# Routing weights of a sinkhorn mixture of experts: the maximum over partitions by two small DMAs, the 1e-9 kept inside the table, and the first output pair's steps spread out

## The chip, the cores and the metric

The kernel runs on one core of a Trainium2 chip. A core has TensorE (PE in the profile; its weight loads are the row PEld), VectorE (DVE), ScalarE (ACT), GpSimd (POOL) and the sync engine (SP), whose queue issues DMAs. Each engine works through its own queue in order and waits on semaphores for the others. SBUF is the on-chip memory of 128 partitions; PSUM holds what TensorE writes, in banks of 512 fp32 values per partition. The metric is the device time of one execution in microseconds, the median of the runs; lower is better.

## The reference, cut to what matters

Attention with a sorted key and value order comes first; its output `x` (3072 tokens of 512) goes through eight experts, each token's outputs weighted by a table `P` that is balanced by rows and columns eight times.

```python
def _moe_ref(x, w_gate, w1, w2):
    N, D = x.shape
    E = w_gate.shape[1]
    logits = x @ w_gate
    logits = logits - logits.max()
    P = np.exp(logits)
    for _ in range(8):
        P /= P.sum(1, keepdims=True) + 1e-09
        P /= P.sum(0, keepdims=True) + 1e-09
        P *= N / E
    out = np.zeros((N, D), dtype=np.float32)
    for e in range(E):
        h = np.maximum(x @ w1[e], 0.0)
        ye = h @ w2[e]
        out += P[:, e:e + 1] * ye
    return out.astype(np.float32)
```

N is 3072, E is 8, the hidden width F is 1024. The maximum is over all tokens and experts, and each column sum over all tokens, so both cross the 128 partitions.

## The kernel before

The attention of four batches comes first and lasts until some 123 us. Its matmuls are mixed with those of expert 0, which is computed densely: `expert_hidden` and `expert_out` (line 377) make the unweighted output of expert 0 for a batch's tokens and copy it from PSUM into `osbl`, the output table of 24 tiles of 128 tokens (line 386: tiles 1, 4 and 5 by ScalarE, the others by VectorE). `logits` leaves the gate's logits in `glog`, 128 partitions by 24 tiles by 8 experts.

Then the seven other experts run in a main loop over rounds `r` (line 818). They use a seven-product scheme for 2x2 blocks (Strassen's, in Winograd's form): sums of weight blocks (`sum_w`, `sum_w2`, on GpSimd), of token blocks (`sum_x`) and of hidden blocks (`Pair.sums`, line 702, on GpSimd) are made beforehand. A round has seven steps of the hidden layer, `p1, p5, p6, p2, p7, p3, p4` from `hidden`, each two matmuls of 512 columns (line 601), with copies and relus on ScalarE and two relu-sums on VectorE (line 590, a custom operation). From `r = 5` on a round also has the output steps of a pair of token tiles: `q5, q1, q6, q2, q3` of this round's pair, and `q7, q4` of the pair before, each four matmuls of 256 columns (line 712) and, apart from q1, which is copied by ScalarE (line 723), followed by a `gather` on VectorE (line 662) that multiplies by the routing weight in `glog` and adds to `osbl`. Round 5 is the first with a pair and has no pair before it: the list of its output steps leaves the missing ones out, so its five steps stand behind the first five hidden steps. In rounds 0 to 4 the loop takes the steps of `last_dense` instead: the second half of the last batch's expert 0.

The routing weights come from the generator `balance` (line 550), woven into this. Its table `G` of 192 values per partition lies in PSUM, in the third bank of the ring `oacc`. The maximum of all logits is taken per partition on VectorE (line 558), turned into a row by an fp32 matmul with an identity (559), reduced again (561) and spread to all partitions by a second fp32 matmul with ones (563); then ScalarE takes the exponential (566). Each of eight iterations has a row part on VectorE (572 to 576: sum, add 1e-9, reciprocal, multiply, and the partition's column sums) and a column part: an fp32 matmul with ones that adds over the partitions (578), then on VectorE scale and add (579), reciprocal (581), multiply (582). Every `yield` ends a step.

The order is written by hand. `pin` keeps an instruction at its place on its engine. The string on line 792 says in which order the steps of the dense part (T), of the chain (C) and of `sum_x` (X) are issued before the main loop: a T is one hidden block of 384 tokens (four matmuls, line 776), or half of an output tile (four matmuls, line 784). In the main loop line 862 says behind which hidden steps of rounds 0 to 4 the chain takes a step, and line 849 empties it at round 5. `scale0` (line 753) multiplies a tile of `osbl` by expert 0's weight on ScalarE; it needs the finished `glog`. Line 864 does it for tiles 4 and 0 in round 4; the next tiles follow from round 5 on, two a round.

The output is stored by SP's queue, and only in the last expert (line 667).

Of the kernel before, what the change touches and what calls it, by code (L numbers as in the profile page):

```python
# [13 lines left out]
F32 = mybir.dt.float32  # L14
BF16 = mybir.dt.bfloat16
AF = mybir.ActivationFunctionType
AX = mybir.AxisListType
ALU = mybir.AluOpType


def mkap(t, dims, off=0):
    return bass.AP(tensor=t.tensor, offset=t.offset + off, ap=dims)
# [3 lines left out]
def kernel(  # L26
# [11 lines left out]
    nc = tc.nc  # L38
    B, H, S, D = 4, 8, 768, 64
    NB, BL = 8, 96  # L40
    N, Dm, E, F = 3072, 512, 8, 1024
    NT = 24
# [16 lines left out]
    pin = tc.keep_in_program_order  # L59
# [4 lines left out]
    osbl = xtp.tile([128, NT, Dm], F32)  # L64
    glog = xtp.tile([128, NT, E], F32)
# [21 lines left out]
    def load_w1(e):  # L87
        w1t[e] = wp.tile([128, 4, F], BF16, name="w1e")
        pin(nc.gpsimd.dma_start(out=w1t[e],
                                in_=moe_w1[e].rearrange("(kk k) f -> k kk f", k=128)))  # L90
# [6 lines left out]
    Ibig = ones.tile([128, 128], BF16)  # L97
# [279 lines left out]
    def expert_out(c0, hTs, bank):  # L377
        for tt in range(3):
            oacc = bank()
            for fb in range(8):  # L380
                pin(nc.tensor.matmul(oacc, hTs[:, fb, tt * 128:(tt + 1) * 128],  # L381
                                     w2t[0][:, fb, :], start=(fb == 0), stop=(fb == 7)))
                if fb == 3:
                    yield
            t = c0 // 128 + tt
            (nc.scalar.copy if t in (1, 4, 5) else nc.vector.tensor_copy)(osbl[:, t, :], oacc)
            yield

    def expert0(bb, bank):
# [24 lines left out]
    with tc.tile_pool(name="ps0", bufs=7, space=bass.MemoryType.PSUM,  # L414
# [28 lines left out]
        for eng, i0, n in ((nc.vector.tensor_copy, 0, 5), (nc.scalar.copy, 5, 3)):  # L443
# [3 lines left out]
                                 axis=AX.X))  # L447
# [7 lines left out]
        for h in range(0, 8, 2):  # L455
            nc.vector.tensor_tensor(
                out=Rt[0][:, h:h + 2],
                in0=mkap(pbps, [pbps.ap[0], [1, 2], [32, 8], [0, 16]], off=h),
                in1=mkap(mask16, [mask16.ap[0], [0, 2], [0, 8], [1, 16]]), op=ALU.mult)
# [34 lines left out]
    mpc, xcp, wq, wcq = late("mpc", 1), late("xcp", 1), late("wq", 2), late("wcq", 1)  # L494
# [38 lines left out]
    def sum_x(p, eng, hold=pin):  # L533
        ta, tb = (slice(1024 * p + 512 * i, 1024 * p + 512 * i + 512) for i in range(2))
        b11, b12, b21, b22 = (xtT[:, k:k + 2, t] for k in (0, 2) for t in (ta, tb))
        x1, x2, x4 = (xc[:, j, :, 512 * p:512 * p + 512] for j in range(3))
        for a, b, c in ((b12, b11, x1), (b22, x1, x2), (b21, x2, x4), (b22, b12, b12)):
            for k in ((slice(0, 1), slice(1, 2)) if p == 2 and c is b12 else (slice(0, 2),)):
                hold(eng.tensor_tensor(out=c[:, k], in0=a[:, k], in1=b[:, k],
                                       op=ALU.subtract))  # L540
                yield

    onesc = mpc.tile([128, 128], F32)
    nc.gpsimd.memset(onesc, 1.0)
    I128 = mpc.tile([128, 128], F32)
    nc.scalar.copy(I128, Ibig)
    for _ in sum_x(0, nc.vector, lambda ins: ins):
        pass

    def balance():  # L550

        room = rings["oacc"][2]
        G = room[:, 0:NT * E].rearrange("p (t e) -> p t e", e=E)
        sums = room[:, 192:192 + NT]
        csps = room[:, 256:256 + E]
        gmps = room[:, 384:512]
        gm = mpc.tile([128, 1], F32)
        pin(nc.vector.reduce_max(out=gm, in_=glog.rearrange("p t e -> p (t e)"), axis=AX.X))
        pin(nc.tensor.matmul(gmps[0:1, :], gm, I128, start=True, stop=True))
        gm1 = mpc.tile([1, 1], F32)  # L560
        pin(nc.vector.reduce_max(out=gm1, in_=gmps[0:1, :], axis=AX.X, negate=True))
        yield
        pin(nc.tensor.matmul(csps[:, 0:1], onesc[0:1, :], gm1, start=True, stop=True))
        gneg = mpc.tile([128, 1], F32)
        pin(nc.vector.tensor_copy(gneg, csps[:, 0:1]))
        pin(nc.scalar.activation(out=G, in_=glog, func=AF.Exp, bias=gneg))
        rs2 = mpc.tile([128, NT], F32)
        cs2 = mpc.tile([128, E], F32)
        cs1 = mpc.tile([128, E], F32)
        yield  # L570
        for it in range(8):
            pin(nc.vector.reduce_sum(out=sums, in_=G, axis=AX.X))
            pin(nc.vector.tensor_scalar_add(rs2, sums, 1e-9))
            pin(nc.vector.reciprocal(out=rs2, in_=rs2))
            pin(nc.vector.tensor_mul(G, G, mkap(rs2, [rs2.ap[0], rs2.ap[1], [0, E]])))
            pin(nc.vector.reduce_sum(out=cs2, in_=G.rearrange("p t e -> p e t"), axis=AX.X))
            yield
            pin(nc.tensor.matmul(csps, onesc, cs2, start=True, stop=True))
            pin(nc.vector.tensor_scalar(out=cs1, in0=csps, scalar1=float(E) / N,
                                        scalar2=1e-9 * E / N, op0=ALU.mult, op1=ALU.add))  # L580
            pin(nc.vector.reciprocal(out=cs1, in_=cs1))
            pin(nc.vector.tensor_mul(glog if it == 7 else G, G,
                                     mkap(cs1, [cs1.ap[0], [0, NT], cs1.ap[1]])))
            yield

    TOP = 3.0e38
    relu = lambda o, x: nc.scalar.activation(out=o, in_=x, func=AF.Relu)  # L587
# [165 lines left out]
    def scale0(ts):  # L753
        for t in ts:
            pin(nc.scalar.activation(out=osbl[:, t, :], in_=osbl[:, t, :], func=AF.Copy,
                                     scale=glog[:, t, 0:1]))

    def last_dense():
# [7 lines left out]
        for c in range(2):  # L766
# [14 lines left out]
            for tt in range(3):  # L781
# [7 lines left out]
                yield  # L789

    dense, chain, xs = last_dense(), balance(), sum_x(2, nc.vector)
    for step in "TTCXTTCXTTCXTTCTTCTTT":
        next({"T": dense, "C": chain, "X": xs}[step])
    held_x = mpc.tile([128, 2], BF16)
    pin(nc.gpsimd.tensor_copy(held_x, xc[:, 2, 0, 1024:1026]))
# [16 lines left out]
    for m, o in enumerate(ends):  # L812
        e, p, hT, _ = chunks[-1]
# [4 lines left out]
    for r in range(len(pairs) + 6):  # L818
        n, i = r // 4, r % 4
        if n < C:  # L820
            e, p, hT, s3 = chunks[n]
            if i == 0 and (n == 1 or n > 1 and p == 0) and e + 1 < E:
                load_w1(e + 1)
                queue.append(sum_w(e + 1))
            if r == 5 or p == 1 and i == 2 and n > 1 and e + 1 < E:
                load_w2(2 if r == 5 else e + 1)
            if r == 8 or p == 1 and i == 2 and n > 1 and e + 1 < E:
                queue.append(sum_w2(2 if r == 8 else e + 1))
            steps, rest = hidden(e, p, i, hT, s3, r < 4)
        else:  # L830
            steps, spares, rest = spares[:7], spares[7:], None
        k = r - 5
        if k + 1 in range(len(pairs)):
            pairs[k + 1].sums()
        weights((0, 2, 2, 0, 0)[r] if r < 5 else 2 if r < 12 else 1 + i % 2)
        now = pairs[k] if k in range(len(pairs)) else None
        if r < 5:
            outs = [lambda: next(dense), None, lambda: next(dense), None,
                    lambda: next(dense)]
        else:  # L840
            outs = [getattr(a, b) for a, b in
                    ((now, "q5"), (before, "q7"), (now, "q1"), (before, "q4"),
                     (now, "q6"), (now, "q2"), (now, "q3")) if a]
        if now and now.last:
            plains, steps = iter(steps), []
            outs = [next(plains) if o == "x" else getattr(before if o[1:] else now, "q" + o[0])
                    for o in "5 7' x 1 x 4' 6 x 2 x 7 x x 3 4".split()]
            now = None
        if r == 5:
            for _ in chain:  # L850
                pass
        for j in range(max(len(steps), len(outs))):
            if j < len(steps):
                steps[j]()
                if j == 3 and n < C:
                    if k + 1 in range(1, 12):
                        scale0([8 * ((k + 1) // 4) + (k + 1) % 4 + 4 * m for m in range(2)])
                    if k + 1 in range(len(pairs)):
                        pairs[k + 1].keep()
            if j < len(outs) and outs[j]:  # L860
                outs[j]()
            if r < 5 and j != 3 and (6 * r + j - (j > 3)) % 4 < 2:
                next(chain, 0)
            if r == 4 and j in (2, 5):
                scale0([4 if j == 2 else 0])
            if j == 1 and late:
                late()
                late = None
            if r in (6, 7) and j == 6:
                next(xs)  # L870
        late, before = rest, now
        if n >= C and not spares and not before:
            break
# [30 lines left out]
```

## Time and profile before

| what | us |
|---|---|
| median of 3 runs (lowest, highest) | 664.87 (664.72, 664.96) |
| the profiled execution, its own time | 665.08 |
| span of that execution in the trace | 663.3 |

| engine, over the span | busy us | instructions |
|---|---|---|
| TensorE | 646.5 | 4970 |
| VectorE | 475.1 | 909 |
| ScalarE | 386.8 | 758 |
| GpSimd | 465.8 | 430 |

| stretch, us of the span | TensorE busy | VectorE busy | ScalarE busy | GpSimd busy |
|---|---|---|---|---|
| 121 to 134 (maximum, first iterations, dense) | 12.89 | 7.78 | 5.36 | 3.69 |
| 134 to 162 (rounds 0 to 4) | 27.73 | 20.07 | 20.04 | 21.87 |
| 162 to 168.5 (round 5) | 6.41 | 3.87 | 5.23 | 6.24 |
| 168.5 to 175 (round 6) | 6.45 | 4.72 | 4.94 | 6.34 |

All times in the stretch are from the start of the span. The granted clock of TensorE is 1.00 in all four stretches. A line of a timeline gives the start, the duration, the engine, the line of the kernel, the operation, what it writes and reads with its shape, and how many like it were merged. Matmuls are pipelined: the end of one is modelled and overlaps the next, so gaps on TensorE are read from start to start. A few matmul records are missing from a trace.

### The profile page before, as it was taken

To read this page: it belongs to the slowest core of one execution; us is meant where nothing else is said; L and a number is where in the kernel's file an instruction comes from. 1 tells how busy PE (TensorE), PEld (TensorE's weight loads), DVE (VectorE), ACT (ScalarE), POOL (GpSimd) and SP (SyncE) were. 2 spreads that over 40 slices of the span, in tenths; PEclk is the share of its full clock that TensorE was granted. 3 is DMA by queue.
4 is the path that set the end of the run, shared out by engine and by line. 5 is a ranking of instruction groups with operands and counts; after the bars stand their busy time and mean duration, and the time that the engine had idled before them with its cause. 6 is when DMAs were issued, how large, how long until landed. Compare 5 with 4: busy or idle time off the path is not lost.

```text
span 663.3 us, 13065 instructions
## 1 busy us (share of the span) xinstructions
PE 646.5 (97%) x4970; PEld 422.5 (64%) x5047; DVE 475.1 (72%) x909; ACT 386.8 (58%) x758; POOL 465.8 (70%) x430
## 2 busy tenths in 40 slices
PE   5999999999999999999999999999999999999997
PEld 2555565555666666666666666666666666666665
DVE  7846566666777777777777777777777777777775
ACT  5877657476777755555555555555555655555540
POOL 3543540196999898779796979698797969846641
PEclk9999999999999999999999999999999999999999
DMA  9998944004303040120303040302103040000224
GB/s 151 184 220 138 196 72 65 1 1 71 58 1 64 1 65 1 26 40 3 61 1 65 1 64 2 65 1 38 27 1 64 1 65 2 1 1 33 96 81 174
DMA packets 33743, 36.52 MB, mean 55 GB/s; under 512 B 2064, under 2 KB 27088, under 8 KB 33680
## 3 DMA queue, kind: packets, MB, share of 16 engines
q0 software_dynamic: 26448, 26.81, 25.9%
q1 hardware_dynamic: 6832, 8.38, 4.4%
q8 instruction: 39, 0.64, 0.4%
q10 hardware_dynamic: 400, 0.49, 0.2%
q14 instruction: 24, 0.20, 0.1%
HBM read 52.45 MB, written 6.29 MB: 89 GB/s over the span
## 4 chain that ended last, share of the span: by engine, by line
PE 95%; issue 1%; DVE 1%; ACT 1%; ACTq 0%
PE oacc L712 38%; PE bk L601 36%; PE bank L381 5%; PE bank L368 5%; PE bank L220 1%; PE bank L261 1%; PE oacc L784 1%; PE bk L678 1%; PE bank L243 1%; PE bank L196 1%; PE bk L776 1%; PE bank L146 1%; PE oacc L776 1%; PE bk L784 1%; PE bank L181 0%
## 5 line engine op out<-in xcount | busy, mean ns | idle before, releaser
L662 DVE SCALAR_TENSOR_TENSOR osbl<-oacc,glog,osbl 128x256 f32<-128x256 f32 (+1 forms) x411 | 219.2, 534 | 125.0 <-PE oacc L712 115.7
L587 ACT ACTIVATE hT<-bk 128x512 bf16<-128x512 f32 (+1 forms) x176 | 104.2, 592 | 147.5 <-PE bk L601 130.1
L601 PE MATMUL bk<-xtT,w1e 128*128 128x512 bf16 x478 | 143.5, 379 | 0.9
L712 PEld LDWEIGHTS <-hs 128*128 128x128 bf16 x984 | 96.3, 98 | 62.9 <-issue 0.3
L712 PEld LDWEIGHTS <-hT 128*128 128x128 bf16 x904 | 88.4, 98 | 57.9 <-issue 0.6
L702 POOL TENSOR_TENSOR hs<-hT 128x512 bf16<-128x512 bf16 x82 | 95.1, 1159 | 39.9 <-DVE hT L590 34.4
L712 PE MATMUL oacc<-w2e,hT 128*128 128x256 bf16 x764 | 114.6, 273 | 0.6
L702 POOL TENSOR_TENSOR hs<-hs,hT 128x512 bf16<-128x512 bf16 x82 | 94.6, 1154 | 6.4
L702 POOL TENSOR_TENSOR hs<-hT,hs 128x512 bf16<-128x512 bf16 x82 | 94.6, 1153 | 6.4
L601 PE MATMUL bk<-xc,wc 128*128 128x512 bf16 x317 | 95.2, 379 | 0.1
L712 PE MATMUL oacc<-w2e,hs 128*128 128x256 bf16 x616 | 92.4, 273 | 0.7
L601 PEld LDWEIGHTS <-w1e 128*128 128x128 bf16 x672 | 65.8, 98 | 11.6 <-issue 0.3
L590 DVE CUSTOM_DVE_ANT_0 hT<-bk,p 128x512 bf16<-128x512 f32 x84 | 58.1, 691 | 7.7 <-PE bk L601 3.1
L636 ACT COPY p<-bk 128x512 f32<-128x512 f32 x84 | 49.2, 585 | 24.3 <-PE bk L601 21.0
L630 ACT COPY u<-bk 128x512 f32<-128x512 f32 x84 | 49.2, 586 | 22.2 <-PE bk L601 19.5
L621 ACT COPY bk<-bk 128x512 f32<-128x512 f32 x84 | 48.0, 572 | 20.5 <-PE bk L601 20.5
L590 DVE CUSTOM_DVE_ANT_0 hT<-bk,u 128x512 bf16<-128x512 f32 x84 | 57.1, 680 | 1.6 <-PE bk L601 0.6
L712 PE MATMUL oacc<-w2s,hs 128*128 128x256 bf16 x368 | 55.2, 273 | 0.3
L601 PEld LDWEIGHTS <-wc 128*128 128x128 bf16 x504 | 49.3, 98 | 8.0 <-issue 0.2
L655 DVE SCALAR_TENSOR_TENSOR s<-bk,hT 128x512 bf16<-128x512 f32 x80 | 54.4, 680 | 0.0
L601 PE MATMUL bk<-xtT,wc 128*128 128x512 bf16 x160 | 48.2, 379 | 0.4
L601 PE MATMUL bk<-xc,w1e 128*128 128x512 bf16 x158 | 47.8, 379 | 0.0
(140 smaller groups left out, 827.9 us busy)
## 6 DMA issues: line engine op xcount, KB each, us to landing
w2e<-in_moe_w_dram POOLq DMA_DIRECT2D x8, 1024.0 KB, 9.5
w1e<-in_moe_w_dram POOLq DMA_DIRECT2D x7, 1024.0 KB, 8.3
out_dram<-osbl SPq DMA_DIRECT2D x21, 256.0 KB, 2.0
vsb<-vs SPq DMA_DIRECT2D x25, 96.0 KB, 3.3
vt<-in_v_dram POOLq DMA_DIRECT2D x3, 768.0 KB, 12.3
qt<-in_q_dram POOLq DMA_DIRECT2D x4, 384.0 KB, 10.5
kt<-in_k_dram POOLq DMA_DIRECT2D x4, 384.0 KB, 12.3
kt<-in_k_dram POOLq DMA_DIRECT2D x2, 768.0 KB, 14.4
```

What stands on the lines that cost most here:

```text
L368: pin(nc.tensor.matmul(hps[:, 0:n], w1t[0][:, kk, fb * 128:(fb + 1) * 128], xtT[:, kk, c0:c0 + n], start=(kk == 0), stop=(kk == 3)))
L381: pin(nc.tensor.matmul(oacc, hTs[:, fb, tt * 128:(tt + 1) * 128], w2t[0][:, fb, :], start=(fb == 0), stop=(fb == 7)))
L587: relu = lambda o, x: nc.scalar.activation(out=o, in_=x, func=AF.Relu)
L590: return nc.vector._custom_dve(TENSOR_ADD_SAT, out=o, in0=x, in1=y, s0=TOP, s1=0.0)
L601: pin(nc.tensor.matmul(ps, wa[:, kk, :], xa[:, kk, :], start=(first and kk == 0), stop=(kk == 1), skip_group_check=True))
L621: pin(nc.scalar.copy(t["w"], t["u"]))
L630: pin(nc.scalar.copy(t["u2"], t["u"]))
L636: pin(nc.scalar.copy(t["p5"], t["v"]))
L655: pin(nc.vector.scalar_tensor_tensor(out=s3[:, i, :], in0=t["w"], scalar=0.0, in1=c12, op0=ALU.max, op1=ALU.subtract))
L662: pin(nc.vector.scalar_tensor_tensor(out=o, in0=ps, scalar=glog[:, t, e:e + 1], in1=o, op0=ALU.mult, op1=ALU.add))
L702: pin(nc.gpsimd.tensor_tensor(out=s[:, c], in0=a, in1=b, op=o))
L712: pin(nc.tensor.matmul(ps, h[:, fb, :], w[:, fb, :], start=(first and fb == 0), stop=(fb == 3), skip_group_check=True))
```

## The change

The maximum over partitions no longer goes through TensorE: one DMA on SP's queue writes the 128 partial maxima as a row into one partition, VectorE reduces it, and a second DMA spreads the result to 128 partitions. The identity `I128` goes.

The table in PSUM gets a ninth column that holds 1e-9 and a 25th row that holds 1e-9/128, set once. The row sums run over nine columns, the column sums over 25 rows, so the two additions go as separate instructions. The factor N/E moves into the multiplication by the column's reciprocal, now a scalar_tensor_tensor. The `yield` behind the column part goes: a step is now a column part with the next row part.

The order changes with it: a new string before the main loop, one chain step behind every fourth hidden step in rounds 0 to 3, expert 0's tiles 16 and 17 copied by ScalarE, and the scaling of tile 0 in round 5 instead of round 4. Round 5's output steps keep the places that they have in later rounds, with empty places for the missing ones.

```diff
-            (nc.scalar.copy if t in (1, 4, 5) else nc.vector.tensor_copy)(osbl[:, t, :], oacc)
+            (nc.scalar.copy if t in (1, 4, 5, 16, 17) else nc.vector.tensor_copy)(osbl[:, t, :], oacc)
...
-    I128 = mpc.tile([128, 128], F32)
-    nc.scalar.copy(I128, Ibig)
...
-        G = room[:, 0:NT * E].rearrange("p (t e) -> p t e", e=E)
-        sums = room[:, 192:192 + NT]
+        GE = room[:, 0:(NT + 1) * (E + 1)].rearrange("p (t e) -> p t e", e=E + 1)
+        G = GE[:, 0:NT, 0:E]
         csps = room[:, 256:256 + E]
-        gmps = room[:, 384:512]
         gm = mpc.tile([128, 1], F32)
-        pin(nc.vector.reduce_max(out=gm, in_=glog.rearrange("p t e -> p (t e)"), axis=AX.X))
-        pin(nc.tensor.matmul(gmps[0:1, :], gm, I128, start=True, stop=True))
+        gmr = mpc.tile([1, 128], F32)
         gm1 = mpc.tile([1, 1], F32)
-        pin(nc.vector.reduce_max(out=gm1, in_=gmps[0:1, :], axis=AX.X, negate=True))
-        yield
-        pin(nc.tensor.matmul(csps[:, 0:1], onesc[0:1, :], gm1, start=True, stop=True))
         gneg = mpc.tile([128, 1], F32)
-        pin(nc.vector.tensor_copy(gneg, csps[:, 0:1]))
-        pin(nc.scalar.activation(out=G, in_=glog, func=AF.Exp, bias=gneg))
...
+        pin(nc.vector.reduce_max(out=gm, in_=glog.rearrange("p t e -> p (t e)"), axis=AX.X))
+        pin(nc.sync.dma_start(out=gmr, in_=gm))
+        pin(nc.vector.memset(GE[:, 0:NT, E:E + 1], 1e-9))
+        pin(nc.vector.memset(GE[:, NT, 0:E], 1e-9 / 128))
         yield
+        pin(nc.vector.reduce_max(out=gm1, in_=gmr, axis=AX.X, negate=True))
+        pin(nc.sync.dma_start(out=gneg, in_=mkap(gm1, [gm1.ap[0], [0, 128], [1, 1]])))
+        yield
+        pin(nc.scalar.activation(out=G, in_=glog, func=AF.Exp, bias=gneg))
         for it in range(8):
-            pin(nc.vector.reduce_sum(out=sums, in_=G, axis=AX.X))
-            pin(nc.vector.tensor_scalar_add(rs2, sums, 1e-9))
+            pin(nc.vector.reduce_sum(out=rs2, in_=GE[:, 0:NT], axis=AX.X))
             pin(nc.vector.reciprocal(out=rs2, in_=rs2))
             pin(nc.vector.tensor_mul(G, G, mkap(rs2, [rs2.ap[0], rs2.ap[1], [0, E]])))
-            pin(nc.vector.reduce_sum(out=cs2, in_=G.rearrange("p t e -> p e t"), axis=AX.X))
+            pin(nc.vector.reduce_sum(out=cs2, in_=GE[:, :, 0:E].rearrange("p t e -> p e t"),
+                                     axis=AX.X))
             yield
             pin(nc.tensor.matmul(csps, onesc, cs2, start=True, stop=True))
-            pin(nc.vector.tensor_scalar(out=cs1, in0=csps, scalar1=float(E) / N,
-                                        scalar2=1e-9 * E / N, op0=ALU.mult, op1=ALU.add))
-            pin(nc.vector.reciprocal(out=cs1, in_=cs1))
-            pin(nc.vector.tensor_mul(glog if it == 7 else G, G,
-                                     mkap(cs1, [cs1.ap[0], [0, NT], cs1.ap[1]])))
-            yield
+            pin(nc.vector.reciprocal(out=cs1, in_=csps))
+            pin(nc.vector.scalar_tensor_tensor(
+                out=glog if it == 7 else G, in0=G, scalar=float(N) / E,
+                in1=mkap(cs1, [cs1.ap[0], [0, NT], cs1.ap[1]]), op0=ALU.mult, op1=ALU.mult))
...
-    for step in "TTCXTTCXTTCXTTCTTCTTT":
+    for step in "CXXTTTTCXTTCTTTTCTTTC":
...
+        elif r == 5:
+            outs = [now.q5, None, now.q1, None, now.q6, now.q2, now.q3]
...
-            if r < 5 and j != 3 and (6 * r + j - (j > 3)) % 4 < 2:
+            if r < 4 and j != 3 and (6 * r + j - (j > 3)) % 4 == 3:
                 next(chain, 0)
-            if r == 4 and j in (2, 5):
-                scale0([4 if j == 2 else 0])
+            if (r, j) in ((4, 2), (5, 2)):
+                scale0([4 if r == 4 else 0])
```

## The prediction

> **What bounds the kernel now.** I read the shares and the chain of waits first, then the timelines of TensorE (PE), VectorE (DVE) and ScalarE (ACT) from 121 to 175 us, the stretch the diff touches, then the DMA issues.
>
> ```profile
> PE 646.5 (97%) x4970; PEld 422.5 (64%) x5047; DVE 475.1 (72%) x909; ACT 386.8 (58%) x758; POOL 465.8 (70%) x430
> ...
> PE 95%; issue 1%; DVE 1%; ACT 1%; ACTq 0%
> ```
>
> PE is busy 97% and is 95% of the chain that ends last. After 168 us its timeline shows no gap but missing records (one 512-column matmul, 0.216 us, at a time). So time counts only if it leaves PE's own queue, and what PE gains before 168 us it keeps to the end. Four kinds of loss stand in the stretch. First, the fp32 matmuls that spread the logits' maximum:
>
> ```profile
> 123.66 1.46 PE L776 MATMUL bk<-xtT,w1e 128*128 128x384 bf16 x8
> 125.05 0.38 PE L559 MATMUL oacc<-I,gm 128*1 128x128 f32 x2
> 125.36 1.48 PE L776 MATMUL bk<-xtT,w1e 128*128 128x384 bf16 x8
> 126.77 0.38 PE L563 MATMUL oacc<-gm,onesc 1*128 1x1 f32 x2
> 127.08 2.77 PE L776 MATMUL bk<-xtT,w1e 128*128 128x384 bf16 x16
> ```
>
> A 384-column matmul starts every 0.1625 us (16 in 127.08 to 129.69). Eight from 123.66 would end at 124.96; the next group starts at 125.36, so L559 costs 0.40. The same way L563 costs 127.08 - 126.66 = 0.42.
>
> Second and third, PE waiting for the routing chain on DVE, and the chain's length:
>
> ```profile
> 139.98 0.15 DVE L579 TENSOR_SCALAR cs<-oacc 128x8 f32<-128x8 f32 x1
> 140.17 0.20 DVE L581 RECIPROCAL cs<-cs 128x8 f32<-128x8 f32 x1
> 140.41 0.37 DVE L582 TENSOR_TENSOR oacc<-oacc,cs 128x192 f32<-128x192 f32 x1
> 140.81 0.37 DVE L572 TENSOR_REDUCE oacc<-oacc 128x24 f32<-128x192 f32 x1
> 141.21 0.18 DVE L573 TENSOR_SCALAR rs<-oacc 128x24 f32<-128x24 f32 x1
> 141.42 0.30 DVE L574 RECIPROCAL rs<-rs 128x24 f32<-128x24 f32 x1
> 141.76 0.37 DVE L575 TENSOR_TENSOR oacc<-oacc,rs 128x192 f32<-128x192 f32 x1
> 142.16 0.36 DVE L576 TENSOR_REDUCE cs<-oacc 128x8 f32<-128x192 f32 x1
> ...
> 142.57 0.39 PE L578 MATMUL oacc<-cs,onesc 128*128 128x8 f32 x2
> ```
>
> PE's previous group (141.64, four of 384 columns) ended at 142.29; L578 starts 0.05 after L576 ends. PE lost 0.28 here and 0.07 before the L578 at 146.34.
>
> Fourth, the first output pair (round r = 5 of the main loop):
>
> ```profile
> 162.56 0.60 PE L712 MATMUL oacc<-w2s,hs 128*128 128x256 bf16 x4
> 163.21 0.59 PE L601 MATMUL bk<-xc,wc 128*128 128x512 bf16 x2
> 163.81 0.60 PE L712 MATMUL oacc<-w2e,hT 128*128 128x256 bf16 x4
> 164.24 0.59 PE L601 MATMUL bk<-xc,wc 128*128 128x512 bf16 x2
> 164.85 0.60 PE L712 MATMUL oacc<-w2s,hs 128*128 128x256 bf16 x4
> ```
>
> Four of 256 columns take 0.435, two of 512 take 0.43. Gaps: 0.21 before 163.21, 0.17 before 163.81, 0.18 before 164.85, and 0.18 before 167.63: 0.74 in sum. Rounds from r = 6 on, which have seven output steps instead of five packed to the front, have none.
>
> **The change, part by part.**
> *Maximum by two DMAs.* Both fp32 matmuls leave PE: 0.40 + 0.42 = **0.82 gained**; nothing replaces them on PE. What hides the DMAs: on DVE two 0.69 copies (t = 16, 17) leave, one of them ahead of the logits' copy, so the maximum is ready some 0.5 earlier, near 122.7. In the built program's order the exp stands on ACT behind the sixth relu of the dense group. That group ends at 123.66 + 6 x 0.65 = 127.56; a relu starts 0.21 after its group and takes 0.49, so the exp cannot start before 128.26. From 122.7 the two DMAs, a 0.28 reduction (L561's row) and about 0.15 of issue and wake-up have 5.1 us for the pair. The rows:
>
> ```profile
> vsb<-vs SPq DMA_DIRECT2D x25, 96.0 KB, 3.3
> ...
> P<-in_sort_net_dram SPq DMA_DIRECT2D x1, 8.0 KB, 1.6
> glog<-in_moe_w_gate_dram SPq DMA_DIRECT2D x1, 16.0 KB, 1.8
> ```
>
> The new ones move 512 bytes in 4-byte pieces. Nearest are 8 KB (1.6) and 16 KB in 32-byte pieces (1.8); upper row 3.3, SBUF to SBUF. I take 1.8 each: 3.6 of 5.1, hidden. At 3.3 each the exp is 1.5 late; the relus of groups seven and eight queue behind it, and the chain is late too; the first column matmul has 0.3 slack, so PE would lose 1.2. On SP's queue the last earlier DMA was issued near 95 us and the output stores come hundreds of us later: nothing is queued behind. On DVE the second reduction waits for the first DMA with one sum_x operation behind it, which the held-over copy on POOL (130.23 before) follows; it comes earlier, near 126.
>
> *Copies t = 16, 17 on ACT.* 2 x 0.59 into ACT's 5.62 us idle before 124.56: nothing. Without that cover the first relu would be up to 0.6 late. The removed cast of I128 (0.315 on ACT at 105) gets no credit.
>
> *The 1e-9 in the table.* Column and row sums take it along; L573 and L579 go, the factor N/E moves into a scalar_tensor_tensor. From L579 to the end of L576 an iteration is 2.54 us (130.08 to 132.62). Without the pitches of L579 (0.19) and L573 (0.22) it is 2.13. The sums run over 216 and 200 elements instead of 192; by the copies L386 (512 elements, 0.69) and L281 (48, 0.20) an element costs 1.06 ns, so +0.03: 2.16. The last multiply keeps 0.37, as L655 (same operation, 512, 0.68) minus 320 elements gives 0.34. The rows of G are now 9 apart; L576 already reads with a step of 8 and takes 0.36, as the contiguous L572. With 0.32 from the matmul's start to DVE's next operation (135.47 to 135.79) and 0.05 back, a loop from matmul to matmul is 2.53.
>
> *Steps merged and spaced.* Column and next row part are one step now. I counted PE's work between the eight column matmuls in the built order (0.15 each). From first to second 12 x 0.216 = 2.59, slack to the loop 0.2; to the third 4.32, ample; to the fourth 8 x 0.216 + 0.65 = 2.38, slack 2.38 + 0.15 - 2.53 = 0: a tie; to the fifth 3.46; sixth 4.11; seventh 2.59, slack 0.2; eighth 3.89. Following DVE as well: in round 1 the relu-sum (L590, 0.69) that frees p4's bank stands behind a whole 2.16 step, and PE reaches p4 some 0.14 early. New waits I take as 0.09 + 0.14 = 0.23 against 0.35 before: **0.1 gained**. Bounds: with 0.03 off each of the six operations the new waits vanish (gain 0.35); with 0.05 on each, five places wait, 1.2 in all (loss 0.85).
>
> *Round 5.* q1 waits for q5's gather, p-steps wait for ACT copies; the gather and copies get a whole 0.43 step more between them, and the scaling of tile 0 (L755, 0.72) leaves round 4, where it stood ahead of the relu at 162.57. It needs glog from the chain, whose last step ends in round 3 now. Following ACT, 0.1 of the 0.74 stays: **0.63 gained**; bounds 0 and 0.74. POOL must keep up: pair 1's sums (L702) ended at 167.20, used at 168.49, slack 1.29, more than the 0.63; and the relu-sum that released POOL at 157.95 no longer waits behind a row part. Without that cover the next pair's q5 would wait the difference.
>
> Sum: 0.82 + 0.10 + 0.63 = 1.55. The profiled execution was 665.08 (span 663.3 and 1.8 around it), the median 664.87: 0.2 apart. Span 661.75, profiled 663.5, median **663.3**.
>
> **Rivals.**
> A. *Merged steps dearer.* DVE operations on the 9-step table cost 0.05 more each, or the merged step blocks relu-sums longer: 0.82 - 0.85 + 0.63 = 0.6 gained, 664.3. For: two slacks of 0.2 and a tie; a 0.05 change decides. Against: L576 pays nothing for its step.
> [...]
> B. *Spacing idle.* Round 5's waits come from ACT's load (5.23 of the 6.5 us from 162), not from the order, and stay: 0.92 gained, 663.95.
> C. *Slower: the DMAs on one engine.* If the 128 4-byte pieces go one after another, at the mean packet of SP's queue (4.4% of 16 engines' 663.3 us over 6832 packets, 0.068 us), each DMA is 1.6 + 8.7 = 10.3. PE waits 20.6 - 5.4 = 15, time near 678. It eats the whole gain from a pair of 5.4 + 1.55 = 7.0 us on. For: no DMA like it runs here. Against: the 16 KB row's 512 pieces of 32 bytes landed in 1.8.
> [...]
> D. *No new waits at all*: 0.82 + 0.35 + 0.74 = 1.91, 662.95.
>
> **How the numbers follow.** Forecast 0.45, D 0.15, A 0.17, B 0.13, C 0.05, and 0.05 for a loss of more than 0.2% by some chain wait. The likeliest one's own range is 663.0 to 663.9. The range reaches from below D to A with dearer operations and 3.3 us DMAs: 662.6 to 665.0. What a measurement of this kernel can tell from no change, 0.2%, is 1.33 us. Below 663.54 lie D and most of the forecast's share: 0.58; within it A, B and the rest: 0.35; slower than 666.2: 0.07.
>
> **What would show it.** No fp32 matmul among the first eight dense groups, which then last 5.2 us; both DMAs landing in about 2 us and the exp following the sixth relu at once; PE gaps only near the fourth column matmul and p4 of round 1, together below 0.3; round 5 about 5.2 us long with gaps of 0.1. Wrong if ACT's exp waits for the DMA, if the six DVE rows exceed 0.37, or if round 5 keeps its gaps.

## The result and the profile after

The changed kernel takes 662.92 us (median of 9 runs, 662.54 to 664.29), the kernel before 665.06 beside it (9 runs, 664.58 to 665.93): a ratio of 0.9969, 95% interval 0.9960 to 0.9978. The profiled execution took 662.94 with a span of 661.2, against 665.08 and 663.3.

The page after, with the busy times and the engine shares of the chain that ended last:

```profile
PE 648.5 (98%) x5043; PEld 421.9 (64%) x5043; DVE 471.2 (71%) x892; ACT 388.1 (59%) x759; POOL 466.0 (70%) x430
...
PE 96%; DMA 2%; POOL 1%; DVE 0%; issue 0%; POOLq 0%
```

TensorE was the bound and still is. Its busy time is higher although two matmuls went, because fewer records are missing from this trace (5043 for 4970, beside 5043 and 5047 weight loads). What can be compared is a stretch from start to start: from the first dense group (L776 before, now L773) to the first output step of round 6. It was 44.83 us (123.66 to 168.49) and is 42.79 (123.69 to 166.48): 2.04 us shorter, and from there to the end both kernels differ by 0.1.

The timeline of the changed kernel at the maximum (start, duration, engine, line, operation):

```profile
122.46 0.35 DVE L561 TENSOR_REDUCE gm<-glog 128x1 f32<-128x192 f32 x1
123.69 5.36 PE L773 MATMUL bk<-xtT,w1e 128*128 128x384 bf16 x32
124.84 0.27 DVE L566 TENSOR_REDUCE gm<-gmr 1x1 f32<-1x128 f32 x1 [0.49 <-DMA gmr<-gm]
127.79 0.49 ACT L584 ACTIVATE hT<-bk 128x384 bf16<-128x384 f32 x1 [0.16 <-PE bk L773]
128.18 0.42 ACT L569 ACTIVATE oacc<-glog,gneg 128x192 f32<-128x192 f32 x1
128.89 1.89 PE L781 MATMUL bk<-w2e,hT 128*128 128x512 bf16 x8
```

All 32 matmuls of the dense block now run without a break, and the next group starts 5.20 after the first. The exp (L569) follows the sixth relu at once. Its bias came by the two DMAs; their issues and landing times, from the views by tile:

```profile
L562 SPq DMA_DIRECT2D gmr<-gm x1: 548/548/548, 122.8 to 122.8; - x1
...
DMA to landing us min/median/max: 2.0/2.0/2.0
L567 SPq DMA_DIRECT2D gneg<-gm x1: 549/549/549, 125.1 to 125.1; - x1
...
DMA to landing us min/median/max: 2.4/2.4/2.4
```

The second was issued at 125.1 and landed near 127.5, 0.6 to 0.7 before the exp could start anyway.

The timeline of the changed kernel around the fourth column matmul, TensorE and VectorE:

```profile
139.89 0.59 PE L598 MATMUL bk<-xc,wc 128*128 128x512 bf16 x2
139.95 0.37 DVE L574 TENSOR_REDUCE cs<-oacc 128x8 f32<-128x200 f32 x1
140.23 0.68 DVE L587 CUSTOM_DVE_ANT_0 hT<-bk,u 128x512 bf16<-128x512 f32 x1
140.37 0.39 PE L577 MATMUL oacc<-cs,onesc 128*128 128x8 f32 x2
...
140.83 0.20 DVE L578 RECIPROCAL cs<-oacc 128x8 f32<-128x8 f32 x1
141.06 0.37 DVE L579 SCALAR_TENSOR_TENSOR oacc<-oacc,cs 128x192 f32<-128x192 f32 x1
141.46 0.38 DVE L571 TENSOR_REDUCE rs<-oacc 128x24 f32<-128x216 f32 x1
141.88 0.30 DVE L572 RECIPROCAL rs<-rs 128x24 f32<-128x24 f32 x1
142.22 0.37 DVE L573 TENSOR_TENSOR oacc<-oacc,rs 128x192 f32<-128x192 f32 x1
142.62 0.37 DVE L574 TENSOR_REDUCE cs<-oacc 128x8 f32<-128x200 f32 x1
142.90 0.68 DVE L587 CUSTOM_DVE_ANT_0 hT<-bk,p 128x512 bf16<-128x512 f32 x1
143.20 0.59 PE L598 MATMUL bk<-xtT,wc 128*128 128x512 bf16 x2
143.64 0.59 PE L598 MATMUL bk<-xc,w1e 128*128 128x512 bf16 x2
```

The iteration has six VectorE operations and is 2.16 long (140.83 to 142.99). PE waits 0.05 before L577 and at no other column matmul; p4 (143.64) follows p3's group of 143.20 without a gap, since the relu-sum that frees its bank (started at 142.90) ended 0.06 before.

Round 5, TensorE alone:

```profile
161.24 0.60 PE L709 MATMUL oacc<-w2s,hs 128*128 128x256 bf16 x4
161.68 1.06 PE L598 MATMUL bk<-xc,wc 128*128 128x512 bf16 x4
162.58 0.60 PE L709 MATMUL oacc<-w2e,hT 128*128 128x256 bf16 x4
163.01 1.03 PE L598 MATMUL bk<-xtT,w1e 128*128 128x512 bf16 x4
163.88 0.60 PE L709 MATMUL oacc<-w2s,hs 128*128 128x256 bf16 x4
...
166.48 0.60 PE L709 MATMUL oacc<-w2s,hs 128*128 128x256 bf16 x4
```

From 161.24 to 166.48 it is 5.24 long; of the 0.74 of gaps 0.04 is left.

### The profile page after: what moved, and what is told of

Its sections match the earlier page's. It is cut to its first block, busy times and chain, and to the rows that moved or that the text cites. A ratio compares the mean times of both kernels' runs of the same rounds, so it can differ in the third digit from the quotient of the medians.

```text
span 661.2 us, 13122 instructions
## 1 busy us (share of the span) xinstructions
PE 648.5 (98%) x5043; PEld 421.9 (64%) x5043; DVE 471.2 (71%) x892; ACT 388.1 (59%) x759; POOL 466.0 (70%) x430
## 4 chain that ended last, share of the span: by engine, by line
PE 96%; DMA 2%; POOL 1%; DVE 0%; issue 0%; POOLq 0%
PE bk L598 38%; PE oacc L709 38%; PE bank L381 5%; PE bank L368 5%; DMA kt<-in_k_dram 2%; PE bank L220 1%; PE bank L261 1%; PE oacc L781 1%; PE bk L675 1%; PE bank L243 1%; PE bank L196 1%; PE oacc L773 1%; PE bk L773 1%; PE bank L146 1%; PE bk L781 1%; PE bank L181 0%
## 5 line engine op out<-in xcount | busy, mean ns | idle before, releaser
L598 PE MATMUL bk<-xtT,w1e 128*128 128x512 bf16 x504 | 148.9, 379 | 0.0
L699 POOL TENSOR_TENSOR hs<-hT 128x512 bf16<-128x512 bf16 x82 | 95.1, 1160 | 37.1 <-DVE hT L587 31.6
L598 PE MATMUL bk<-xc,wc 128*128 128x512 bf16 x336 | 99.3, 379 | 0.0
L699 POOL TENSOR_TENSOR hs<-hs,hT 128x512 bf16<-128x512 bf16 x82 | 94.6, 1154 | 6.4
L699 POOL TENSOR_TENSOR hs<-hT,hs 128x512 bf16<-128x512 bf16 x82 | 94.6, 1153 | 6.4
L598 PE MATMUL bk<-xc,w1e 128*128 128x512 bf16 x168 | 50.0, 379 | 0.0
L598 PE MATMUL bk<-xtT,wc 128*128 128x512 bf16 x168 | 50.0, 379 | 0.0
```

Of the source, the lines that this page charges most:

```text
L598: pin(nc.tensor.matmul(ps, wa[:, kk, :], xa[:, kk, :], start=(first and kk == 0), stop=(kk == 1), skip_group_check=True))
L699: pin(nc.gpsimd.tensor_tensor(out=s[:, c], in0=a, in1=b, op=o))
```

## The experiments

The theory at this point: three parts each took away PE time of their own (the maximum 0.82, the chain 0.52, round 5 0.70, which make 2.04), and they add up. The rival is that some of them hang together: that a part alone gives nothing or less, because what it frees is lost at the next place. So the parts were undone one by one, and done alone.

In the table "stretch" is from the first dense group to round 6 as above; "to round 8" goes two rounds further. Between the profiled executions the start of the first dense group, which no edit moves by design, lies anywhere from 123.1 to 124.5, so the times of single parts scatter by some tenths, and the stretch is the finer measure. Each ratio is to runs of the kernel before taken beside the version, whose medians lie between 664.90 and 665.06.

| kernel | stretch | to round 8 | median us | ratio to before, interval |
|---|---|---|---|---|
| before | 44.83 | 56.99 | 664.9 | |
| after | 42.79 | 54.95 | 662.92 | 0.9969 (0.9960, 0.9978) |
| max_on_pe | 43.62 | 55.77 | 664.01 | 0.9984 (0.9976, 0.9993) |
| packed_r5 | 43.47 | 55.67 | 663.36 | 0.9976 (0.9966, 0.9986) |
| scale_r4 | 43.02 | 55.59 | 663.80 | 0.9985 (0.9972, 0.9997) |
| adds_back | 44.77 | 56.93 | 664.89 | 0.9987 (0.9969, 1.0004) |
| adds_psum | 44.16 | 56.32 | 664.60 | 1.0001 (0.9985, 1.0017) |
| hop_more | 43.70 | 55.85 | 664.41 | 1.0000 (0.9986, 1.0014) |
| spacing_only | 44.15 | 56.78 | 665.08 | 1.0002 (0.9993, 1.0011) |
| spacing_moved | 44.13 | 56.29 | 664.67 | 0.9997 (0.9988, 1.0006) |
| table_only | 44.22 | 56.38 | 664.33 | 0.9991 (0.9983, 1.0000) |
| bf16_cols | 42.11 | 54.27 | 662.13 | 0.9960 (0.9948, 0.9973) |
| after_again | 42.79 | 54.94 | 662.95 | 0.9968 (0.9957, 0.9979) |
| bf16_again | 42.11 | 54.27 | 662.10 | 0.9956 (0.9943, 0.9969) |

### max_on_pe: the maximum through TensorE again

```diff
-        pin(nc.sync.dma_start(out=gmr, in_=gm))
...
-        pin(nc.vector.reduce_max(out=gm1, in_=gmr, axis=AX.X, negate=True))
-        pin(nc.sync.dma_start(out=gneg, in_=mkap(gm1, [gm1.ap[0], [0, 128], [1, 1]])))
+        pin(nc.tensor.matmul(gmps[0:1, :], gm, I128, start=True, stop=True))
+        pin(nc.vector.reduce_max(out=gm1, in_=gmps[0:1, :], axis=AX.X, negate=True))
+        yield
+        pin(nc.tensor.matmul(csps[:, 0:1], onesc[0:1, :], gm1, start=True, stop=True))
+        pin(nc.vector.tensor_copy(gneg, csps[:, 0:1]))
...
-    for step in "CXXTTTTCXTTCTTTTCTTTC":
+    for step in "CXXTTCXTTCTTCTTTTCTTTC":
```

> The changed kernel with the maximum spread by the two fp32 matmuls again, all else kept. Theory: TensorE pays 0.40 + 0.42 again, the stretch is 42.79 + 0.82 = 43.6 and the time 0.8 above the changed kernel. Rival (the matmuls only filled time that TensorE then waits for the chain, which starts with the exponential behind the sixth relu in both): 42.8 and no change of time.

The string has one C more, for the step that the second matmul opens. The stretch grows by 0.83. The two matmuls cost here what they cost before (0.41 each, for 0.40 and 0.42), so taking them off TensorE brings all of it.

### packed_r5 and scale_r4: the two halves of round 5's edit

packed_r5 puts the five output steps behind the first five hidden steps again; there tile 0 is scaled after its first product was added, so that product is also multiplied by expert 0's weight.

```diff
-            outs = [now.q5, None, now.q1, None, now.q6, now.q2, now.q3]
+            outs = [now.q5, now.q1, now.q6, now.q2, now.q3]
```

> The changed kernel with round 5's five output steps packed behind the first five hidden steps again, the scaling of tile 0 left in round 5. Theory (the order makes the gaps): TensorE waits 0.6 to 0.7 again in round 5, the stretch is 43.4 and the time 0.6 above the changed kernel. Rival (ScalarE's scaling in round 4 made them): the gaps do not come back, 42.8.

scale_r4 keeps the order and scales tile 0 in round 4 again.

```diff
-            if (r, j) in ((4, 2), (5, 2)):
-                scale0([4 if r == 4 else 0])
+            if r == 4 and j in (2, 5):
+                scale0([4 if j == 2 else 0])
```

> The changed kernel with the scaling of tile 0 on ScalarE in round 4 again, ahead of round 5's copies; the spread order of round 5 stays. Theory: the order removed nearly all of round 5's waits and the scaling a small part, so about 0.2 comes back at the first product of round 5: stretch to round 6 42.9 to 43.1 (after 42.79). Rival: the scaling ahead of the relu was the cause of the waits, and the 0.7 comes back: 43.4 or more.

Packing brings 0.68 of the 0.70 back: PE waits 0.38, 0.18 and 0.18, where the kernel before has 0.21 and 0.17 close together, 0.18 and 0.18. Tile 0's scaling stands in round 5 all the same, so the order alone is enough for these waits. The scaling alone brings back 0.23, at the first product. The two overlap (0.68 and 0.23 are more than 0.70). The timeline of scale_r4 shows how:

```profile
160.16 0.73 ACT L752 ACTIVATE osbl<-osbl,glog 128x512 f32<-128x512 f32 x1
160.78 0.60 PE L709 MATMUL oacc<-w2s,hs 128*128 128x256 bf16 x4
160.79 0.59 ACT L584 ACTIVATE hT<-bk 128x512 bf16<-128x512 f32 x1
161.26 0.60 ACT L618 COPY bk<-bk 128x512 f32<-128x512 f32 x1
161.42 1.08 PE L598 MATMUL bk<-xc,wc 128*128 128x512 bf16 x4
```

The scaling ends at 160.89 on ScalarE, the relu and the copy behind it are late, and PE's group of 161.42 starts 0.64 after the one before it, which needs 0.435. To round 8 scale_r4 loses another 0.42, in round 7; spacing_only shows why.

### spacing_only and spacing_moved: round 5 alone on the kernel before

```diff
+        elif r == 5:
+            outs = [now.q5, None, now.q1, None, now.q6, now.q2, now.q3]
...
-            if r == 4 and j in (2, 5):
-                scale0([4 if j == 2 else 0])
+            if (r, j) in ((4, 2), (5, 2)):
+                scale0([4 if r == 4 else 0])
```

> The kernel before with only round 5's output steps spread and tile 0's scaling moved to round 5. Read on TensorE from the first dense group after the attention to the first output step of round 6: 44.83 us before, 42.79 after the whole change. Theory (three separate losses on TensorE add up): round 5's gaps go alone, 44.83 - 0.70 = 44.1, and the time is 0.7 below the kernel before. Rival (the spacing helps only because the chain ends earlier in the changed kernel): the tile weights are late, the gaps stay, 44.8 and no change of time.

The gaps of round 5 go and the stretch shortens by 0.68, and yet the time does not change. PE waits anew: 0.48 of it is lost in round 7, and another 0.20 later. The timeline of spacing_only in round 7:

```profile
173.99 1.15 POOL L411 TENSOR_TENSOR wc<-w1e,wc 128x512 bf16<-128x512 bf16 x1
174.10 1.33 DVE L539 TENSOR_TENSOR xtT<-xtT 128x512 bf16<-128x512 bf16 x1
175.10 1.33 POOL L702 TENSOR_TENSOR hs<-hT 128x512 bf16<-128x512 bf16 x1
175.35 0.86 DVE L662 SCALAR_TENSOR_TENSOR osbl<-oacc,glog,osbl 128x256 f32<-128x256 f32 x2
175.87 0.60 PE L712 MATMUL oacc<-w2e,hT 128*128 128x256 bf16 x4 [0.32 <-DVE osbl L662]
```

One VectorE subtraction with two SBUF inputs (L539, the token-block sums) takes 1.33. It started 0.11 after a GpSimd operation, and ended 0.29 after that one's end (175.14). The gather behind it is late and PE waits for the gather. The same subtraction in the changed kernel started just ahead of GpSimd:

```profile
173.00 0.41 DVE L539 TENSOR_TENSOR xtT<-xtT 128x512 bf16<-128x512 bf16 x1
173.07 1.36 POOL L699 TENSOR_TENSOR hs<-hT 128x512 bf16<-128x512 bf16 x1
```

It takes 0.41, and GpSimd's operation is the longer one, 1.36 for the usual 1.15. The durations between follow the same pattern: the subtraction took 0.62 in the kernel before and 0.78 in packed_r5, and there too it ended 0.28 to 0.29 after the GpSimd operation that was under way. Of the two operations in these rows the one that starts later stands still for most of what is left of the other: the subtraction's 1.33 is 0.92 over its 0.41, with 1.04 of GpSimd's operation left when it started (174.10 to 175.14), and GpSimd's 1.36 is 0.21 over its 1.15, with 0.34 of the subtraction left (173.07 to 173.41). What in the chip makes them wait for each other, no run shows.

The other 0.20 is lost in two places far behind: 0.11 before the hidden step of 288.45 and 0.09 before that of 483.05, each starting 0.05 after a relu-sum (L590) ends. So nothing is left of the 0.68: from the first dense group to the last output step (658.79, and 659.00 before) it is 535.35 here and 535.34 in the kernel before. Why those two relu-sums come late was not looked into.

To test this, spacing_moved is spacing_only with that VectorE subtraction of rounds 6 and 7 (and nothing else) at another place: if the meeting with GpSimd's operation costs the 0.48, the stretch to round 8 is 56.78 - 0.48 = 56.30. The expectation calls it the weight-block sums; what line 871 moves are the token-block sums of L539.

```diff
-            if r in (6, 7) and j == 6:
+            if r in (6, 7) and j == 2:
                 next(xs)
```

> The kernel before with round 5's output steps spread and tile 0's scaling in round 5, and, in rounds 6 and 7, the next pair's weight-block sums taken at the third hidden step instead of the seventh. [...] Rival: the order of the spread steps itself costs the time in round 7; then the wait of about 0.3 to 0.5 before an output step of round 7 stays, and the stretch stays at 56.8.

The two subtractions take 0.65 and 0.43, the wait in round 7 is gone, and the stretch to round 8 is 56.29, the 56.30 of the meeting and not the rival's 56.8. The time fell short of it: 0.2 below before, where that stretch is 0.70 shorter, with an interval up to 1.0006. The two late waits are here too (0.09 before 288.95 and 0.11 before 483.57), so that 0.50 of the 0.70 is left at the last output step (534.84 from the first dense group, for 535.34). In the profiled execution the first dense group also started 0.8 later than before (124.46 for 123.66), ahead of all that was edited; what varies there was not looked into. So the meeting and its cost are shown on the trace, and no gain in the time that would answer to it.

In scale_r4 the same operation again took 1.27, behind another GpSimd operation, for a loss of 0.42. In max_on_pe, table_only, adds_psum and hop_more it took 0.41 to 0.45 at the same place in the source: which engine comes first there is a matter of a few tenths of a us.

### table_only: the ninth column and the 25th row alone

```diff
+        GE = room[:, 0:(NT + 1) * (E + 1)].rearrange("p (t e) -> p t e", e=E + 1)
+        G = GE[:, 0:NT, 0:E]
...
-            pin(nc.vector.reduce_sum(out=sums, in_=G, axis=AX.X))
-            pin(nc.vector.tensor_scalar_add(rs2, sums, 1e-9))
+            pin(nc.vector.reduce_sum(out=rs2, in_=GE[:, 0:NT], axis=AX.X))
...
-            pin(nc.vector.tensor_scalar(out=cs1, in0=csps, scalar1=float(E) / N,
-                                        scalar2=1e-9 * E / N, op0=ALU.mult, op1=ALU.add))
-            pin(nc.vector.reciprocal(out=cs1, in_=cs1))
+            pin(nc.vector.reciprocal(out=cs1, in_=csps))
```

The multiplication and the column sum change as in the whole change; order, steps and maximum stay.

> The kernel before with the 1e-9 as a column and a row of the table alone: maximum by matmuls, order and steps as before. Theory: an iteration is 0.38 us shorter, so the two waits of the chain before its column matmuls (0.28 and 0.07) go, and a column matmul that is not waited for costs TensorE 0.14 instead of 0.24: stretch to round 6 44.3 to 44.4 (before 44.83), round 5 keeps its gaps. Rival: the saving comes of the new order alone, and the stretch stays at 44.8. A second rival: rows of nine cost VectorE time on the old order, and the waits stay or grow.

The stretch shortens by 0.61: the waits of 0.28 and 0.07 are gone, and the eight column matmuls cost 1.18 in sum for 1.44 before (0.35 + 0.26). A column matmul stands as two passes in the trace (x2; in bf16, below, as one); where PE had to wait for it, the first pass takes 0.13 before the second starts, where the operand had been there for 0.24 or longer 0.03, and where it came only 0.10 to 0.13 ahead 0.05 to 0.09; the second takes 0.11. A wait thus costs 0.10 more than its gap.

### adds_back and adds_psum: the additions as instructions again

```diff
-            pin(nc.vector.reduce_sum(out=rs2, in_=GE[:, 0:NT], axis=AX.X))
+            pin(nc.vector.reduce_sum(out=rs2, in_=G, axis=AX.X))
+            pin(nc.vector.tensor_scalar_add(rs2, rs2, 1e-9))
...
-            pin(nc.vector.reciprocal(out=cs1, in_=csps))
+            pin(nc.vector.tensor_scalar_add(cs1, csps, 1e-9))
+            pin(nc.vector.reciprocal(out=cs1, in_=cs1))
```

> The changed kernel with the two additions of 1e-9 as instructions of their own again (eight VectorE operations an iteration, sums over 192), order kept. Theory (the loop from column matmul to column matmul, 2.53, has slacks of 0 to 0.2 at three places): 0.41 more a loop makes TensorE wait some 0.25, 0.45, 0.5, 0.25 and 0.1, together 1.3 more, the stretch 44.1 and the time 1.3 above the changed kernel. Rival (VectorE is busy 71%, so two short operations are hidden): 42.8 to 42.9.

The stretch grew by 1.98, more than an addition's length explains, and the reason lies in the edit: the row sums stand in SBUF here, and some of the additions on them take far longer than 0.18. The timeline of adds_back:

```profile
131.68 1.15 POOL L528 TENSOR_TENSOR w2s<-w2e,w2s 128x512 bf16<-128x512 bf16 x1
132.32 0.54 DVE L572 TENSOR_SCALAR rs<-rs 128x24 f32<-128x24 f32 x1
```

The addition from SBUF to SBUF ended at 132.86, right after GpSimd's operation (132.83); the longest of the eight took 1.45, the shortest 0.18. The four that took 0.40 or more all ended 0.03 to 0.04 after a GpSimd operation, and the two with no GpSimd operation under way took 0.18. That looks like the same standing still, on an operation with a single input. Not every operation from SBUF to SBUF shows it: the reciprocal behind the addition took 0.30 each time, beside a running GpSimd operation too (129.45, inside 129.34 to 130.49). So adds_psum puts the sums in PSUM, as the kernel before has them.

```diff
+        sums = room[:, 232:232 + NT]
...
+            pin(nc.vector.reduce_sum(out=sums, in_=G, axis=AX.X))
+            pin(nc.vector.tensor_scalar_add(rs2, sums, 1e-9))
```

> The changed kernel with the two additions of 1e-9 as instructions of their own again, the row sums in PSUM as before (the table keeps its ninth column and 25th row, which nothing reads). Theory: each iteration of the chain is 0.4 us longer, the merged steps have no room for it, and TensorE waits at five column matmuls, 1.2 to 1.6 us in all: stretch from the first dense group to round 6 44.0 to 44.4 (after 42.79), and both additions take 0.15 to 0.2 us each, unlike the 0.5 and 1.45 with the sums in SBUF. Rival: the chain has the room, and only the fourth column matmul waits: 42.8 to 43.1.

All eight additions take 0.18 now, and the stretch grows by 1.37. PE waits at three column matmuls and at p4 of round 1 (0.20, 0.44, 0.20 and 0.38). The timeline of adds_psum at the second and last of these:

```profile
140.56 0.36 DVE L576 TENSOR_REDUCE cs<-oacc 128x8 f32<-128x192 f32 x1
140.97 0.39 PE L579 MATMUL oacc<-cs,onesc 128*128 128x8 f32 x2 [0.27 <-DVE cs L576]
...
143.81 0.59 PE L601 MATMUL bk<-xtT,wc 128*128 128x512 bf16 x2
144.62 0.59 PE L601 MATMUL bk<-xc,w1e 128*128 128x512 bf16 x2 [0.22 <-DVE hT L590]
```

In the old order the two additions cost 0.61 (table_only), in the new one 1.37: the merged steps have room for six operations and not for eight. Here the parts do hang together.

### hop_more: one more DMA in the chain

```diff
+        pin(nc.sync.dma_start(out=gnew, in_=gneg))
         yield
-        pin(nc.scalar.activation(out=G, in_=glog, func=AF.Exp, bias=gneg))
+        pin(nc.scalar.activation(out=G, in_=glog, func=AF.Exp, bias=gnew))
```

> The changed kernel with a third small DMA in the chain of the maximum, which copies the spread maximum once more before the exp reads it. Theory: the two DMAs are hidden by only 0.6 us (the second lands near 127.5, the exp stands behind a relu until 128.18), so a third of 2.0 to 2.4 us makes the exp 1.4 to 1.8 late; it holds up the last two relus of the dense block and the first column matmul, and TensorE loses 1.0 to 1.5: stretch from the first dense group to round 6 43.8 to 44.3 (after 42.79). Rival: transfers here are hidden anyway, by the work between the maximum and the first column matmul; 42.8.

The third DMA landed in 1.7, and the timeline of hop_more shows the exp wait for it:

```profile
129.38 0.42 ACT L571 ACTIVATE oacc<-glog,gnew 128x192 f32<-128x192 f32 x1 [1.05 <-DMA gnew<-gneg]
...
131.50 0.36 PE L579 MATMUL oacc<-cs,onesc 128*128 128x8 f32 x2 [0.47 <-DVE cs L576]
```

The exp is 1.15 late (the dense group starts 0.05 later too), the stretch grows by 0.91. This is a little under the range expected, since the DMA was faster than the other two; the rival, that transfers cost nothing here, falls. Two DMAs fit and three do not.

### bf16_cols, bf16_again, after_again: what the column matmuls themselves cost

bf16_cols rounds each partition's column sums, and the ones, to bf16; the sums over the partitions are then of rounded values.

```diff
-    onesc = mpc.tile([128, 128], F32)
+    onesc = mpc.tile([128, 128], BF16)
...
-        cs2 = mpc.tile([128, E], F32)
+        cs2 = mpc.tile([128, E], BF16)
```

> The changed kernel with the partitions' column sums and the matrix of ones in bf16, so that the column matmul runs in bf16 (the column sums are rounded to bf16 before they are added over the partitions). Theory: the eight column matmuls cost TensorE 1.22 us in the changed kernel since they are fp32; in bf16 each costs 0.03 to 0.06, 0.7 to 1.0 less in sum: stretch to round 6 41.8 to 42.1 (after 42.79), time about 0.8 below the changed kernel. Rival: the 0.14 of such a matmul is the switch between kinds of work and the 0.1 that of a wait, which bf16 does not change: 42.6 to 42.8.

> The version with the column sums and the ones in bf16, unaltered, beside the changed kernel: stretch to round 6 42.1, and 0.7 below the changed kernel in time. If the gain seen before was a matter of the chip or of the attention's start, the two come out within 0.2 of each other.

> The changed kernel, unaltered, beside the version with the column matmul in bf16: stretch to round 6 42.8 and 662.9 us, as before.

Both runs of it give 42.11, 0.68 less than the changed kernel. On the same chip its five times (661.98 to 662.21) all lie below the seven of the changed kernel (662.33 to 663.71), the medians 0.85 apart. Each column matmul costs 0.03, 0.22 in sum for 1.22; that is 1.00 saved. A third of it is given back. The timeline of bf16_again:

```profile
139.39 0.59 PE L599 MATMUL bk<-xc,wc 128*128 128x512 bf16 x2
139.95 0.17 PE L578 MATMUL oacc<-cs,onesc 128*128 128x8 bf16 x1
...
142.48 0.68 DVE L588 CUSTOM_DVE_ANT_0 hT<-bk,p 128x512 bf16<-128x512 f32 x1
142.57 0.59 PE L599 MATMUL bk<-xtT,wc 128*128 128x512 bf16 x2
143.22 0.59 PE L599 MATMUL bk<-xc,w1e 128*128 128x512 bf16 x2
```

PE comes 0.13 too early to the fourth column matmul (139.95 - 139.39 - 0.43) and 0.22 too early to p4 (143.22 - 142.57 - 0.43), whose relu-sum ends at 143.16. With 0.03 more ahead of p4 in round 0 the waits are 0.38 here, for 0.05 in the changed kernel: 1.00 - 0.33 = 0.67. This is the fastest version that was run, at the price of the rounded sums. Whether a later place for two chain steps wins the 0.38 back was not tried.

## Why the prediction came out as it did

The forecast was 663.3 and the kernel takes 662.92. That lies inside the stated range (662.6 to 665.0), 0.08 below the 663.0 to 663.9 that the forecast gave for itself, and beside rival D's 662.95, which had a chance of 0.15. Every part went the way that was worked out; two terms of the sum were too small. That the time meets D's is luck in part: D has no waits at all left and nothing for the column matmuls, while 0.05 and 0.04 of waits were left and 0.22 came from the column matmuls, which is how its 1.91 became the 2.04 of the trace.

- *Maximum by two DMAs, 0.82.* Measured 0.83. The cover was read rightly: the exp stands behind the sixth relu (128.18, forecast 128.26), and the maximum was ready at 122.81 (forecast near 122.7). The DMAs were mis-sized, 2.0 and 2.4 for 1.8 each; the first one's reduction and the two issues included, 0.6 of the cover was left, and hop_more shows that it ends there. Rival C, 10.3 us for a DMA of 128 pieces, is far from the 2.0 and 2.4 measured.
- *Copies 16 and 17 on ScalarE, nothing.* The first relu started at 124.59, 0.25 after its group for the usual 0.21. That the cover would hold without this edit was not tried.
- *The table, six operations, 2.16 from reciprocal to column sum.* Measured 2.16, and 2.56 from one column matmul to the next that waits (137.81 to 140.37), forecast 2.53. The step of nine costs nothing: 0.37 for both multiplications and for the 200-element column sum, 0.38 for the 216-element row sum. Rival A's dearer rows did not occur.
- *Chain waits, 0.10.* This is the term that was mis-sized: 0.52 was gained. Of the new waits, put at 0.09 and 0.14, the fourth column matmul had 0.05 and p4 none, by a margin of 0.06: 0.30 gained where the sum has 0.10. The other 0.22 stands in no term of the sum: counted to the start of the next matmul, the eight column matmuls took 1.22 for 1.44. One of them was waited for instead of two, which is 0.10; two whose operand had come only 0.12 to 0.13 ahead were 0.05 dearer together; and 0.06 was a wait of p4 in round 0 behind the third (139.27), for a relu-sum that ended at 139.22. The wait at p4 of round 1 was rightly placed and mis-sized: as soon as PE is quicker by the fp32 passes, it is there, 0.22 in bf16_again. How much of the margin the longer waited matmul gives, and how much that VectorE starts the relu-sum 0.09 before L574's end, the runs do not tell.
- *Round 5, 0.63.* Measured 0.70, and packed_r5 puts it down to the order; rival B, ScalarE's load alone, falls, though scale_r4 shows 0.23 of load. GpSimd's cover held: pair 1's sums (L699) ended at 164.96 and were used at 166.48, a slack of 1.52 for 1.29 before.
- *"What PE gains before 168 us it keeps to the end."* True of this change (from the first dense group to the last output step 533.30 for 535.34, the same 2.04), and not as a rule: spacing_only and scale_r4 gave 0.48 and 0.42 back in round 7, where VectorE stood still behind GpSimd. No rival of the prediction had this. With the two late waits of 0.20 it takes away all that round 5's edit gains when it is made alone.

As for the whole: the maximum's 0.83, the table's 0.61 on the old order and round 5's 0.68 make 2.12, against 2.04 for all together. The new order and the merged steps bring nothing of their own beyond that. What they may be worth is that the exp comes 0.8 later (128.18 for 127.38) and all together still falls short of the sum by only 0.08; what the old order would have made of that exp was not run.

## What to carry to other kernels

When TensorE is the bound, tiny fp32 matmuls that move a value across partitions are worth removing: two of them cost 0.82 and eight column sums 1.22, while two dependent 512-byte DMAs took 4.4 us and none of the bound's time, because the consumer stood behind other work for longer than that. Find the instruction that the consumer queues behind and count the cover up to its end; here 0.6 us of it was left. And before a gain early in a steady pipeline is counted to the end, look for pairs of VectorE and GpSimd operations that start close together: a shift of a few tenths decides which of them stands still, 0.41 or 1.33 us here for the same subtraction.

## What the runs showed of the hardware that was not expected

- A VectorE operation with two bf16 SBUF inputs (128x512) takes 0.41 when it starts first, and 1.33 or 1.27 when a GpSimd operation has just started, ending 0.28 to 0.29 after it; a 24-element addition from SBUF to SBUF took 0.18 to 1.45, from PSUM 0.18 each time. GpSimd's 1.15 became 1.36 when VectorE came first.
- An fp32 matmul of 8 columns costs PE 0.14 when its operand has been there for 0.24 or longer and 0.24 when PE waited for it; in bf16 0.03.
- Small DMAs from SBUF to SBUF on SP's queue landed in 2.0 (a column into one row), 2.4 (one value to 128 partitions) and 1.7 (a column to a column), though each writes 512 bytes.
